# Half-pieces in a hand-interleaved attention and MLP kernel: attention steps counted behind each half of an MLP piece, with a new list of allowances

## The chip, the cores and the metric

One core of one Trainium2 chip runs the whole kernel. The metric is the device time of one execution in microseconds (us). TensorE does the matrix products (PE in the profile; its weight loads are PEld), VectorE (DVE) and ScalarE (ACT) do the elementwise work, GpSimd (POOL) some more of it, and SyncE (SP) mostly issues DMAs.

## What is computed

The reference runs a normalised attention and then an MLP block on its output:

```
q_n, k_n = rmsnorm(q, g_q), rmsnorm(k, g_k)          # (8 batches, 12 heads, 448 tokens, 64)
attn = softmax(q_n @ k_n.T / 8) @ v                  # per batch and head
x = attn, heads side by side                         # (8, 448, 768)
xn = layernorm(x) * g_ln
out = x + relu(xn @ w_ch1) @ w_ch2                   # w_ch1 768 x 3072, w_ch2 3072 x 768
```

## The kernel before

The attention of batch 0 runs first, in an order written out by hand (`ORDER`). After that come eight stages. In stage b (b = 0 to 7) TensorE runs the MLP of batch b and, in between, the attention of batch b + 1; stage 7 has only the MLP. The instructions of each engine run in the order in which Python emits them; nothing reorders them.

**The attention steps.** `attention` (line 529) makes a list of steps, 42 for each stage. Heads are taken in pairs, six pairs to a batch, seven steps to a pair. A step of index i holds the scores of one pair, `scores(p, i)`, and the values of the pair before it, `values(p - 1, i)`. A score step (written S below) is one matmul of 448 columns into a PSUM bank (line 397), which ScalarE turns into E with an exponential (line 413). A value step (V) is four small matmuls of E with v into the banks oA and oB (lines 450 and 452). Step 1 holds two value steps, step 6 the seventh (V6). After V6, `evac_o` (lines 465 to 472) divides on VectorE and frees oA and oB; there is one of each, so the next pair's first V waits for that. The seventh scores of two pairs are made together, as four narrow matmuls into two banks (line 403, written L4). Score banks are two, and from pair 15 (in batch 2) on a third one is used in turn (`score_bank`, line 419). The steps also carry the preparation of later heads: two squares on ScalarE (line 254) and a rounding copy (line 279), sums and scalings on VectorE, DMA transposes and loads on SP.

**The MLP pieces.** `mlp_chunks` yields pieces with a cost. In stages 1 to 7 a piece of the first product ("up", line 775) is 12 matmuls of 256 columns or 24 of 128 columns into one bank, followed by a ReLU on ScalarE (line 777), cost 1280; a piece of the second product (line 797) is 6 matmuls of 384 columns, cost 960. In stage 0 both kinds are 6 matmuls of 384 columns (lines 700 and 711), cost 960. Pieces of cost 0 are VectorE, ScalarE and GpSimd work such as `sums` and `sum3` (line 780), `add` (line 737) and `join` (line 807). An MLP batch is done in two groups: tokens 0 to 255 and then the rest in odd batches, the third block of 128 and then the other two in even batches. The bank pool of the MLP has three buffers.

**The pace.** `run_rest` (line 951) emits one piece, adds its cost to `done`, and then emits attention steps up to `start + (goal - start) * done / (total - 960 * tail)`. `tail` comes from `TAIL` (line 64), so a tail of 17 means that the steps are all out when 17 x 960 of cost is left. Then the layer norm of the next batch follows, one item behind each piece: A (aggregate), N (normalise, on VectorE), X (transpose by DMA, on SP, at the earliest when 10 pieces are left, `DOWN`), R (root). In stages 0 and 1 one of 16 weight sums on VectorE (line 743) also follows a piece, from the last nine pieces of stage 0 on.

Of the kernel before, what the change touches and what calls it, by code (L numbers as in the profile page):

```python
# [8 lines left out]
FP32 = mybir.dt.float32  # L9
# [3 lines left out]
AFT = mybir.ActivationFunctionType  # L13
# [7 lines left out]
NDC, NFF = DM // 128, FF // 128  # L21
# [39 lines left out]
RS_RATIO = 4.0  # L61
HALF, HCOL = NFF // 2, DM // 2
DOWN = 10
TAIL = (13, 17, 17, 17, 17, 17, 17, 0)
FLAG_AT = (6, 30)
E_RING = 9
RING = [(u, n) for u in (4, 6, *range(DMA_UNIT, len(UNITS))) for n in "kq"]
# [20 lines left out]
class _Fast:  # L88
# [603 lines left out]
    def first_mlp(self):  # L692

        nc, sh = self.nc, self.sh
        tiles, xnT, hT = self.tok_tiles(0), self.xnT, self.hS

        def up(f):
            ps = self.ps_m.tile([128, 512], FP32, tag="mlp", name="psH")
            for dc in range(NDC):
                nc.tensor.matmul(ps[:, 0:384], sh.w1[:, dc, ts(f, 128)], xnT[:, dc],  # L700
                                 start=(dc == 0), stop=(dc == NDC - 1))
            nc.scalar.activation(out=hT[:, f], in_=ps[:, 0:384], func=AFT.Relu)

        cur = {}

        def down(t, g, s):
            if s == 0:
                cur["ps"] = self.ps_m.tile([128, 512], FP32, tag="mlp", name="psC")
            ps = cur["ps"][:, 0:HCOL]
            for f in range(6 * s, 6 * s + 6):  # L710
                nc.tensor.matmul(ps, hT[:, f, ts(t, 128)], sh.w2[:, f, ts(g, HCOL)],
                                 start=(f == 0), stop=(f == NFF - 1))
            if s == 3:
                self.add(0, t, g, ps)
                if g and t < 2:
                    self.late.append((0, t, slice(0, DM)))
                elif t == 2:
                    self.store(0, t, slice(g * HCOL, g * HCOL + HCOL))
            elif s == 1:
                self.store_late()  # L720

        for f in range(UP_FIRST, NFF):
            yield 6 * 384 / 2.4, (lambda f=f: up(f))
        for g in range(2):
            for t in range(3):
                for s in range(4):
                    yield 6 * HCOL / 2.4, (lambda t=t, g=g, s=s: down(t, g, s))

    def store_late(self):
        for a in self.late:  # L730
# [23 lines left out]
    def mlp_group(self, b, tiles, end, before=(), after=()):  # L754

        nc, sh = self.nc, self.sh
        w2, w2s, S2 = sh.w2, self.w2s, self.S2
        lo, hi = slice(0, HALF), slice(HALF, NFF)
        t0, n = tiles[0], len(tiles)
        N, k = 128 * n, 4 // n  # L760
        hT = self.hT if n == 2 else self.h1
        last = b == B - 1
        final = last and end
        A1, A2 = (lambda f: hT[:, f, 0:128]), (lambda f: hT[:, f, 128:256])
        B11, B21 = w2[:, lo, 0:HCOL], w2[:, hi, 0:HCOL]
        B22, T3 = w2[:, hi, HCOL:DM], w2[:, lo, HCOL:DM]
        T1, T2, T4 = (w2s[:, i] for i in range(3))
        U, V, W = self.U, self.V, S2.rearrange("p f n -> p (f n)").bitcast(FP32)[:, 0:HCOL]
        bank, half, before = {}, 6 * HCOL / 2.4, list(before)

        def up(f):
            ps = self.ps_m.tile([128, k, N], FP32, tag="mlp", name="psH")
            for i in range(k):
                for dc in range(NDC):
                    nc.tensor.matmul(ps[:, i], sh.w1[:, dc, ts(f + i, 128)], self.xnT[:, dc, 256 - N:256],  # L775
                                     start=(i == 0 and dc == 0), stop=(i == k - 1 and dc == NDC - 1))
            nc.scalar.activation(out=hT[:, f:f + k], in_=ps, func=AFT.Relu)  # L777

        def tt(out, a, c, op=ALU.subtract):
            nc.vector.tensor_tensor(out=out, in0=a, in1=c, op=op)  # L780
# [1 line left out]
        def sum3(i):  # L782
            f = slice(4 * i, 4 * i + 4)
            return 0, lambda: tt(A2(f), A2(f), A1(f))

        def sums(i):
            f, f2 = slice(4 * i, 4 * i + 4), slice(HALF + 4 * i, HALF + 4 * i + 4)
            if n == 1:
                return 0, lambda: tt(S2[:, f], A1(f), A1(f2), ALU.add)
            return 0, lambda: (tt(S2[:, f], A2(f), A2(f2), ALU.add),  # L790
                               tt(A1(f), S2[:, f], A1(f), ALU.add))

        def product(x, a, w, s, start=True, stop=True, c=slice(0, HCOL)):
            if x not in bank:
                bank[x] = self.ps_m.tile([128, 512], FP32, tag="mlp", name="psP")[:, 0:HCOL]
            for f in range(6 * s, 6 * s + 6):
                nc.tensor.matmul(bank[x][:, c], a[:, f], w[:, f, c], start=(start and f == 0),  # L797
                                 stop=(stop and f == HALF - 1))

        run = lambda *a, **kw: [(half, lambda s=s: product(*a, s, **kw)) for s in range(2)]  # L800

        def add(x, t, g):
            return 0, lambda: self.add(b, t0 + t, g, bank[x] if isinstance(x, str) else x)
# [9 lines left out]
                                         nc.scalar if b == B - 1 else nc.gpsimd)  # L813

        for f in range(0, NFF, k):
            yield 6 * 512 / 2.4, (lambda f=f: up(f))
            if before:
                yield 0, before.pop(0)
            if n == 1:
                if f in (16, 20):  # L820
                    yield sums(f // 4 - 4)
                continue
            if f in (4, 8, 12):
                yield sum3(f // 4 - 1)
# [63 lines left out]
            yield done(1)  # L888
            return
        for c in range(0, HCOL, 192):  # L890
            for s in range(2):
                yield half / 2, lambda s=s, c=c: product(f"4{c}", A2(hi), T4, s, c=slice(c, c + 192))
            yield 0, lambda c=c: self.add(b, t0 + 1, 0, bank[f"4{c}"][:, c:c + 192], c, c + 192)
            yield 0, lambda c=c: self.store(b, t0 + 1, slice(c, c + 192), nc.scalar)

# [55 lines left out]
    def run_rest(self):  # L951
        steps, mark, upto = self.steps, self.mark, self.upto
        for b in range(B):
            tail = TAIL[b]
            chunks = list(self.mlp_chunks(b))
            total = sum(c for c, _ in chunks)
            if b + 1 == B:
                for i, (_, emit) in enumerate(chunks):
                    if i == len(chunks) - 55:
                        self.tc.mark_branch_hint_location("general", "LikelyTaken", [ENG.PE, ENG.DVE, ENG.SP, ENG.Activation, ENG.Pool])  # L960
                    emit()
                    if i in FLAG_AT:
                        self.flag(FLAG_AT.index(i))
                break
            start, goal = self.pos, mark[b + 1]
            done, items = 0.0, None
            if b == 0:
                ops, last = self.weight_sums()
            elif b == 1:
                ops += last  # L970
            left = sum(c > 0 for c, _ in chunks)
            for cost, emit in chunks:
                emit()
                if not cost:
                    continue
                left -= 1
# [241 lines left out]
```

## Time and profile before

| | |
|---|---|
| time, median of 3 runs | 590.68 us (589.38 to 590.95) |
| the profiled execution | 591.34 us, of which the span from first to last instruction is 589.8 us |
| TensorE busy | 560.6 us, 95% of the span |
| VectorE, ScalarE, GpSimd busy | 391.3, 373.0, 173.8 us |
| first attention | 0 to 58.6 us of the span |
| stages 0, 1, 2 | from 58.6, 123.2, 197.4 us |
| stages 3, 4, 5 | from 259.9, 333.0, 393.6 us |
| stages 6, 7 | from 466.7, 525.0 us |

The span starts with the first instruction; times inside the profile are counted from there. A busy time of PE joins overlapping matmuls, and a matmul's row is longer than its share of the stream: a matmul of 448 columns has a row of 0.35 us, and the next one starts 0.19 us after it. A PE gap shorter than that overlap does not show as idle time.

### The profile page before, as it was taken

How to read it: one execution, taken by the hardware profiler on the slowest of the kernel's cores; microseconds unless marked ns; L12 is line 12 of the kernel's file. 1: busy time of each engine (PE TensorE's matmuls, PEld its weight loads, DVE VectorE, ACT ScalarE, POOL GpSimd, SP SyncE). 2: the span in 40 equal slices, each digit the busy share in tenths (PEclk: the TensorE clock that was granted, in tenths of full speed). 3: DMA queues.
4: the chain of work that ended last, by engine and by line, in shares of the span. 5: the costliest groups of instructions: out<-in, count | busy, mean ns of one | idle time of the engine just before them, and what ended most of it. 6: DMA issues, size and time to landing. Idle time of an engine off the chain costs nothing.

```text
span 589.8 us, 13476 instructions
## 1 busy us (share of the span) xinstructions
PE 560.6 (95%) x5366; PEld 409.3 (69%) x5366; DVE 391.3 (66%) x832; ACT 373.0 (63%) x693; POOL 173.8 (29%) x196
## 2 busy tenths in 40 slices
PE   3877999999999999999999999999999999999996
PEld 1555566677687867767777767767777777777784
DVE  5798667798768476965868576765868533573424
ACT  5987897448775588738777388738777377323130
POOL 2845433303150511644141421634241410020000
PEclk9999999999999999999999999999999999999999
DMA  8999998839582687959773597949852480030201
GB/s 218 279 209 238 197 208 119 142 110 140 122 129 65 144 123 129 127 140 133 138 118 31 154 137 147 136 126 136 136 90 43 122 107 1 1 108 1 83 0 57
DMA packets 172664, 71.43 MB, mean 121 GB/s; under 512 B 132548, under 2 KB 167556, under 8 KB 172596
## 3 DMA queue, kind: packets, MB, share of 16 engines
q1 hardware_dynamic: 130100, 51.60, 41.5%
q0 software_dynamic: 41552, 18.29, 24.0%
q8 instruction: 43, 0.70, 0.5%
q10 hardware_dynamic: 944, 0.62, 0.5%
q14 instruction: 25, 0.20, 0.1%
HBM read 52.30 MB, written 11.01 MB: 107 GB/s over the span
## 4 chain that ended last, share of the span: by engine, by line
PE 68%; DVE 4%; ACT 2%; DMA 2%; issue 1%; SPq 0%; DVEq 0%; ACTq 0%
PE psP L797 28%; PE psH L775 28%; PE psS L397 5%; PE oA L450 4%; DMA k<-in_k_dram 2%; PE psS L403 1%; PE oB L452 1%; ACT E L413 1%; DVE qn L79 1%; ACT hS L777 1%; DVE ssq L257 1%; DVE x L467 0%; DVE hS L780 0%; ACT khl L254 0%; ACT khl L279 0%
## 5 line engine op out<-in xcount | busy, mean ns | idle before, releaser
L413 ACT ACTIVATE E<-psS,rr_all 128x448 f16<-128x448 f32 x336 | 201.5, 635 | 27.2 <-PE psS L397 23.6
L775 PE MATMUL psH<-xnT,w 128*128 128x256 f16 (+1 forms) x2016 | 216.6, 261 | 0.0
L775 PEld LDWEIGHTS <-w 128*128 128x128 f16 x2016 | 174.8, 98 | 20.5 <-issue 0.9
L777 ACT ACTIVATE hS<-psH 128x512 f16<-128x512 f32 x150 | 90.0, 600 | 121.2 <-PE psH L775 120.5
L797 PEld LDWEIGHTS <-hS 128*128 128x128 f16 x1080 | 100.1, 98 | 62.4 <-issue 5.1
L797 PE MATMUL psP<-w,hS 128*128 128x384 f16 x672 | 123.5, 326 | 0.3 <-DVE x L737 0.3
L397 PE MATMUL psS<-qU,kU 128*128 128x448 f16 x288 | 99.1, 359 | 9.4 <-ACT E L413 6.8
L450 PEld LDWEIGHTS <-E 128*128 128x128 f16 x1008 | 69.8, 98 | 37.5 <-issue 6.3
L271 POOL TENSOR_TENSOR k<-k,gprod 128x896 f32<-128x896 f32 x19 | 40.0, 2105 | 162.5 <-ACT khl L254 107.8
L780 DVE TENSOR_TENSOR hS<-hS 128x512 f16<-128x512 f16 (+1 forms) x119 | 66.1, 563 | 21.2 <-ACT hS L777 19.7
L797 PE MATMUL psP<-w2s,hS 128*128 128x384 f16 (+1 forms) x408 | 70.0, 321 | 0.0
L450 PE MATMUL oA<-v,E 128*128 128x65 f16 x864 | 67.1, 194 | 0.4 <-DVE x L467 0.4
L737 DVE SCALAR_TENSOR_TENSOR x<-psP,rs_all,x 128x384 f32<-128x384 f32 x60 | 36.4, 616 | 31.5 <-PE psP L797 30.2
L452 PE MATMUL oB<-v,E 128*128 128x65 f16 x288 | 52.0, 194 | 0.1
L807 POOL TENSOR_TENSOR x<-x,hS 128x384 f32<-128x384 f32 x21 | 21.4, 1031 | 93.1 <-ACT hS L875 90.9
L465 DVE RECIPROCAL rec_all<-oA 128x6 f32<-128x6 f32 x48 | 9.2, 193 | 58.6 <-PE oA L450 58.5
L212 POOL DMA_DIRECT2D v<-in_v_dram x51 | 39.6, 789 | 6.3 <-PE oB L452 5.4
L397 PEld LDWEIGHTS <-kU 128*128 128x128 f16 x288 | 28.1, 99 | 14.7 <-issue 5.8
L875 ACT ACTIVATE hS<-hS,rs_all 128x384 f32<-128x384 f32 x27 | 14.6, 604 | 33.5 <-DVE hS L780 33.5
L257 DVE TENSOR_REDUCE ssq<-khl 128x14 f32<-128x896 f32 (+1 forms) x24 | 25.5, 1063 | 11.7 <-ACT khl L254 10.8
L452 PEld LDWEIGHTS <-E 128*128 128x128 f16 x336 | 32.7, 97 | 0.5 <-DVE xl L472 0.4
L79 DVE SCALAR_TENSOR_TENSOR qn<-q,rr_all 128x256 f16<-128x256 f32 (+1 forms) x70 | 26.5, 439 | 5.6 <-ACT rr_all L261 5.6
(136 smaller groups left out, 596.3 us busy)
## 6 DMA issues: line engine op xcount, KB each, us to landing
k<-in_k_dram SPq DMA_DIRECT2D x19, 384.0 KB, 4.1
q<-in_q_dram SPq DMA_DIRECT2D x19, 384.0 KB, 3.7
out_dram<-x SPq DMA_DIRECT2D x14, 384.0 KB, 3.0
w<-in_moe_w_ch_dram POOLq DMA_DIRECT2D x3, 1536.0 KB, 14.2
w<-in_moe_w_ch_dram POOLq DMA_DIRECT2D x2, 2304.0 KB, 19.6
out_dram<-x POOLq DMA_DIRECT2D x9, 384.0 KB, 2.9
v<-in_v_dram POOLq DMA_DIRECT2D x51, 64.0 KB, 4.3
qU<-qn SPq DMA_TRANSPOSE x85, 2.6
```

What stands on the lines that cost most here:

```text
L79: nc.vector.scalar_tensor_tensor(out=out, in0=x, scalar=8.0, in1=r.unsqueeze(2).broadcast_to([x.shape[0], g, D]), op0=ALU.mult, op1=ALU.mult)
L212: nc.gpsimd.dma_start(out[:, :, j, 0:D], main[:, :, j])
L271: (nc.vector if u in DVE_KG else nc.gpsimd).tensor_tensor(out=c["t"][1], in0=c["t"][1], in1=sh.gprod.unsqueeze(1).broadcast_to([128, g, D] ...
L397: nc.tensor.matmul(ps[0][:, 0:S], c["main"][:, ts(i, 128)], c["q"][:, ts(h, S)], start=True, stop=True)
L413: nc.scalar.activation(out=o, in_=x[:, 0:S], func=AFT.Exp, scale=self.units[u][3][:, g:g + 1], bias=EXP_BIAS)
L450: nc.tensor.matmul(oA[:, t, cs], E[:, ts(t, 128)], rhs, start=(i == 0 and t == 0), stop=(i == 6 and t == 2))
L452: nc.tensor.matmul(oB[:, cs], E[:, 320:448], rhs, start=(i == 0), stop=(i == 6))
L737: self.nc.vector.scalar_tensor_tensor(out=x, in0=ps, scalar=self.rs[:, b, t:t + 1], in1=x, op0=ALU.mult, op1=ALU.add)
L775: nc.tensor.matmul(ps[:, i], sh.w1[:, dc, ts(f + i, 128)], self.xnT[:, dc, 256 - N:256], start=(i == 0 and dc == 0), stop=(i == k - 1 and ...
L777: nc.scalar.activation(out=hT[:, f:f + k], in_=ps, func=AFT.Relu)
L780: nc.vector.tensor_tensor(out=out, in0=a, in1=c, op=op)
L797: nc.tensor.matmul(bank[x][:, c], a[:, f], w[:, f, c], start=(start and f == 0), stop=(stop and f == HALF - 1))
```

## The change

Each piece with a cost is now a list of two calls, its first and its second half: 6 + 6 or 12 + 12 matmuls of an up piece, 3 + 3 of the others. A half-piece's matmuls stand in the same order and go to the same bank as before. Between the two calls `run_rest` emits attention steps up to the target that belongs to `done + cost / 2`; after the second call it emits up to the same target as before. The ReLU stays behind the second half. `TAIL` goes from 13 to 11 for stage 0, from 17 to 13 for stages 1, 3 and 5, from 17 to 19 for stage 6, and stays at 17 for stages 2 and 4.

```diff
-TAIL = (13, 17, 17, 17, 17, 17, 17, 0)
+TAIL = (11, 13, 17, 13, 17, 13, 19, 0)
...
-        def up(f):
-            ps = self.ps_m.tile([128, k, N], FP32, tag="mlp", name="psH")
-            for i in range(k):
+        def up(f, h):
+            if h == 0:
+                bank["h"] = self.ps_m.tile([128, k, N], FP32, tag="mlp", name="psH")
+            ps = bank["h"]
+            for i in range(h * k // 2, (h + 1) * k // 2):
...
-            nc.scalar.activation(out=hT[:, f:f + k], in_=ps, func=AFT.Relu)
+            if h:
+                nc.scalar.activation(out=hT[:, f:f + k], in_=ps, func=AFT.Relu)
...
-            for f in range(6 * s, 6 * s + 6):
+            for f in range(3 * s, 3 * s + 3):
                 nc.tensor.matmul(bank[x][:, c], a[:, f], w[:, f, c], start=(start and f == 0),
                                  stop=(stop and f == HALF - 1))
...
-            yield 6 * 512 / 2.4, (lambda f=f: up(f))
+            yield 6 * 512 / 2.4, [lambda f=f, h=h: up(f, h) for h in range(2)]
...
             for cost, emit in chunks:
-                emit()
                 if not cost:
+                    emit()
                     continue
+                for i, call in enumerate(emit):
+                    call()
+                    if i + 1 < len(emit):
+                        upto(int(min(goal, start + (goal - start) * (done + cost / 2) / (total - 960 * tail))))
                 left -= 1
```

The same halving is made in `first_mlp` for stage 0. In the last group of stage 7 the four pieces of cost half / 2 become eight of half / 4, with the same matmuls in the same order.

On TensorE the built orders of stages 2, 3 and 6 read as follows (u: up matmuls, p: matmuls of the second product, with their number; S, V and L4 as above; one line for two pairs).

```
stage 2 before  u24 S u24 SVV SV u24 SV SV u24 SVV u24 SSVV u24 SV SV p6 SV SV p6V L4
                p6 S p6 SVV SV p6 SV p6 SV SV p6V p6 SSVV u12 SV SV u12 SV SV u12V L4
                u12 SSVV u12 SV SV u12 SV SV u12V S p6 SVV SV p6 SV u12 SV SV u12V L4
                p12 u36 p60
stage 2 after   u24 S u12 SVV u12 SV u12 SV u12 SV u12 SV u12V u12 S u12 SVV u12 SV u12 SV p3 SV p3 SV p6V L4
                p3 S p6 SVV p3 SV p3 SV p6 SV p3 SV p3V p6 S p3 SVV u6 SV u6 SV u6 SV u6 SV u6V L4
                u12 S u6 SVV u6 SV u6 SV u6 SV u6 SV u6V u6 S p3 SVV p3 SV p6 SV u6 SV u6 SV u6V L4
                u6 p12 u36 p60
stage 3, last pair, before   u12 SSVV u12 SV p6 SV p6 SV u12 SV u12V L4 p12 u36 p60
stage 3, last pair, after    p6 S p6 u6 SVV u6 SV u12 SV p6 SV p6 SV u12V L4 u24 p60
stage 6, last pairs, before  u12 SSVV u12 SV SV u12 SV u12 SVV p6VVV p6V u12VV u12V p12 u36 p60
stage 6, last pairs, after   u6 S u6 SVV u6 SV u6 SV u6 SV u6 SV u6V u6VV u6V u6V p3V p6V p3V u24 p12 u36 p60
```

The order of GpSimd's instructions is the same in both kernels; on SP one DMA transpose of stage 6 stands behind two others instead of before them; VectorE has a few `add` and `sums` at other places among the preparation.

More of the change, by code (lines that the diff above doesn't have):

```diff
@@ L694, in first_mlp, with up @@
         nc, sh = self.nc, self.sh
-        tiles, xnT, hT = self.tok_tiles(0), self.xnT, self.hS
-        def up(f):
-            ps = self.ps_m.tile([128, 512], FP32, tag="mlp", name="psH")
-            for dc in range(NDC):
+        tiles, xnT, hT, cur = self.tok_tiles(0), self.xnT, self.hS, {}
+        def up(f, i):
+            if i == 0:
+                cur["h"] = self.ps_m.tile([128, 512], FP32, tag="mlp", name="psH")
+            ps = cur["h"]
+            for dc in range(3 * i, 3 * i + 3):
                 nc.tensor.matmul(ps[:, 0:384], sh.w1[:, dc, ts(f, 128)], xnT[:, dc],
                                  start=(dc == 0), stop=(dc == NDC - 1))
-            nc.scalar.activation(out=hT[:, f], in_=ps[:, 0:384], func=AFT.Relu)
-        cur = {}
+            if i:
+                nc.scalar.activation(out=hT[:, f], in_=ps[:, 0:384], func=AFT.Relu)
         def down(t, g, s):
@@ L709, in down @@
             ps = cur["ps"][:, 0:HCOL]
-            for f in range(6 * s, 6 * s + 6):
+            for f in range(3 * s, 3 * s + 3):
                 nc.tensor.matmul(ps, hT[:, f, ts(t, 128)], sh.w2[:, f, ts(g, HCOL)],
                                  start=(f == 0), stop=(f == NFF - 1))
-            if s == 3:
+            if s == 7:
                 self.add(0, t, g, ps)
@@ L718, in down @@
                     self.store(0, t, slice(g * HCOL, g * HCOL + HCOL))
-            elif s == 1:
+            elif s == 3:
                 self.store_late()
         for f in range(UP_FIRST, NFF):
-            yield 6 * 384 / 2.4, (lambda f=f: up(f))
+            yield 6 * 384 / 2.4, [lambda f=f, i=i: up(f, i) for i in range(2)]
         for g in range(2):
@@ L726, in first_mlp @@
                 for s in range(4):
-                    yield 6 * HCOL / 2.4, (lambda t=t, g=g, s=s: down(t, g, s))
+                    yield 6 * HCOL / 2.4, [lambda t=t, g=g, s=s: down(t, g, s)
+                                           for s in (2 * s, 2 * s + 1)]
     def store_late(self):
@@ L769, in mlp_group @@
         bank, half, before = {}, 6 * HCOL / 2.4, list(before)
-        def up(f):
-            ps = self.ps_m.tile([128, k, N], FP32, tag="mlp", name="psH")
-            for i in range(k):
+        def up(f, h):
[3 more added lines that the diff above has]
+            for i in range(h * k // 2, (h + 1) * k // 2):
                 for dc in range(NDC):
@@ L795, in product @@
                 bank[x] = self.ps_m.tile([128, 512], FP32, tag="mlp", name="psP")[:, 0:HCOL]
-            for f in range(6 * s, 6 * s + 6):
+            for f in range(3 * s, 3 * s + 3):
                 nc.tensor.matmul(bank[x][:, c], a[:, f], w[:, f, c], start=(start and f == 0),
                                  stop=(stop and f == HALF - 1))
-        run = lambda *a, **kw: [(half, lambda s=s: product(*a, s, **kw)) for s in range(2)]
+        run = lambda *a, **kw: [(half, [lambda s=s: product(*a, s, **kw) for s in (2 * s, 2 * s + 1)])
+                                for s in range(2)]
         def add(x, t, g):
@@ L890, in mlp_group @@
         for c in range(0, HCOL, 192):
-            for s in range(2):
-                yield half / 2, lambda s=s, c=c: product(f"4{c}", A2(hi), T4, s, c=slice(c, c + 192))
+            for s in range(4):
+                yield half / 4, lambda s=s, c=c: product(f"4{c}", A2(hi), T4, s, c=slice(c, c + 192))
             yield 0, lambda c=c: self.add(b, t0 + 1, 0, bank[f"4{c}"][:, c:c + 192], c, c + 192)
@@ L960, in run_rest @@
                         self.tc.mark_branch_hint_location("general", "LikelyTaken", [ENG.PE, ENG.DVE, ENG.SP, ENG.Activation, ENG.Pool])
-                    emit()
+                    for call in emit if isinstance(emit, list) else [emit]:
+                        call()
                     if i in FLAG_AT:
@@ L972, in run_rest @@
             for cost, emit in chunks:
-                emit()
                 if not cost:
+                    emit()
                     continue
+                for i, call in enumerate(emit):
+                    call()
+                    if i + 1 < len(emit):
+                        upto(int(min(goal, start + (goal - start) * (done + cost / 2) / (total - 960 * tail))))
                 left -= 1
```

## The prediction, made before the changed kernel ran

> **What bounds the kernel now.** I read the page's first lines, then busy time by stage, then who makes TensorE wait, then the timelines around the longest waits.
>
> ```profile
> PE 560.6 (95%) x5366; PEld 409.3 (69%) x5366; DVE 391.3 (66%) x832; ACT 373.0 (63%) x693; POOL 173.8 (29%) x196
> ```
>
> TensorE is busy for 95% of the span. The table by stage (length, then PE, PEld, DVE and ACT busy, clock, DMA share) shows where the rest is:
>
> ```profile
> 58.60:123.20 64.60, 63.32 (x547) 40.26 (x545) 47.06 (x99) 44.47 (x85) 22.31 (x23) 1.00 0.97 168
> 123.20:197.40 74.20, 73.61 (x674) 54.27 (x672) 56.14 (x112) 50.41 (x92) 17.91 (x18) 1.00 0.58 109
> 197.40:259.90 62.50, 60.76 (x639) 45.27 (x637) 43.93 (x94) 43.42 (x81) 21.42 (x25) 1.00 0.92 132
> 259.90:333.00 73.10, 73.10 (x673) 54.28 (x672) 49.25 (x102) 49.45 (x91) 24.12 (x27) 1.00 0.64 116
> 333.00:393.60 60.60, 60.06 (x639) 45.03 (x637) 42.00 (x94) 43.44 (x81) 21.79 (x25) 1.00 0.85 136
> 393.60:466.70 73.10, 73.10 (x674) 54.29 (x673) 49.26 (x102) 49.45 (x91) 24.11 (x27) 1.00 0.58 103
> 466.70:525.00 58.30, 58.19 (x628) 43.97 (x627) 28.76 (x74) 32.20 (x60) 8.26 (x12) 1.00 0.32 55
> ```
>
> Length less PE busy is 1.28, 0.59, 1.74, 0, 0.54, 0 and 0.11 us for stages 0 to 6: 4.26 us in all. The change only reorders matmuls in these stages, so this, with about 0.17 us more at each wait (the tail of the last matmul's row, counted as busy), is all it can win. Stages 3 and 5, whose allowance it alters, have nothing to give. The waits of stages 0 to 6 by cause:
>
> ```profile
> PE psS L397 <- ACT E L413: 2.1, 5, 0.5
> PE psS L397 <- DVE kU L365: 0.9, 1, 0.9
> PE oA L450 <- DVE x L467: 0.4, 1, 0.4
> PE psP L797 <- DVE x L737: 0.3, 1, 0.3
> ```
>
> Half is score steps that wait for a bank, which an exponential frees. Stage 2, first PE and then ACT:
>
> ```profile
> 210.04 0.19 PE L452 MATMUL oB<-v,E 128*128 128x65 f16 x1
> 210.78 0.35 PE L397 MATMUL psS<-qU,kU 128*128 128x448 f16 x1 [0.54 <-ACT E L413]
> ```
>
> ```profile
> 206.39 0.60 ACT L777 ACTIVATE hS<-psH 128x512 f16<-128x512 f32 x1 [0.76 <-PE psH L775]
> 206.89 0.94 ACT L254 ACTIVATE khl<-k 128x896 f32<-128x896 f32 x1
> 207.73 0.63 ACT L413 ACTIVATE E<-psS,rr_all 128x448 f16<-128x448 f32 x1
> 208.24 0.95 ACT L254 ACTIVATE qn<-q 128x896 f32<-128x896 f32 x1
> 210.07 0.65 ACT L413 ACTIVATE E<-psS,rr_all 128x448 f16<-128x448 f32 x1
> ```
>
> ScalarE sits idle for 0.76 us until a ReLU's matmuls are done; then two squares and the exponentials come behind it, and the sixth S finds no bank: it starts 0.71 us after the exponential that frees one. From the 210.04 row V's last matmul should be followed after 0.03 us, so the wait is 0.70 us of the stream. Starts in sequence give ACT's rate: an exponential every 0.52, a square or rounding copy 0.85, a ReLU 0.48 us. PE: S 0.19, V 0.12, twelve up matmuls 1.31 (0.67 at 128 columns), three p 0.49.
>
> **The change part by part.** Splitting costs no instruction: matmul counts, order and banks of the MLP stay. An alternation is free: where the timelines change between up, S, V and p without a wait, the next matmul starts on schedule (S at 209.77, V at 209.96). What moves is the place of S and V, on average a quarter piece earlier, and with them their DVE, ACT, SP and POOL work. GpSimd's order stays. On SP one transpose of xn (1.2 us) of stage 6 comes behind two others; group 2 needs it eight p pieces (8 x 0.97 us) later, so I count nothing; without that cover it would cost those two, 2.5 us.
>
> 1. Stages 2 and 4, second pair: S steps no longer come as SVSV but 0.67 and 0.49 us apart, and the ReLU ahead of the squares comes earlier. Walking the new order by the rates above, ACT begins the squares about 1.5 us earlier and every bank is free in time: -0.70 each, **-1.4**.
> 2. The same stages, next boundary: V6 L4 p3 S p6 S V has p3 where p6 stood. V waits for evac_o, behind the rounding copy's followers on VectorE (1.09 and 1.08 us rows); 0.49 us less cover, up to 0.35 late: **+0.7** (0 to +0.7).
> 3. Stage 2, fourth pair. Here ACT waits for a load:
>
> ```profile
> 223.39 0.95 ACT L254 ACTIVATE qn<-q 128x896 f32<-128x896 f32 x1 [1.43 <-DMA k<-in_k_dram]
> ```
>
> The load's issue hangs on an SP chain from the stage's start, not on PE. S steps that come earlier only meet the same late square. Before, waits here cost 0.70 and 0.15; by the walk the fifth S then waits 1.55 and L4 0.56: at most +1.26; 0 if the load lands earlier as well. I take nearer the walk, **+0.9**.
> 4. End of stage 2: L4's second bank 0.36 late becomes 0.2, and the p that waited 0.51 for an add has six more up matmuls (0.65) ahead of it: **-0.7**.
> 5. Stage 4, pairs 4 and 6: the same loads, now just late: 0 to +0.6, **+0.4**.
> 6. Stage 1: a bank wait of 0.34 goes (S spaced by u6). The V at 135.69 waits 0.52 and its oB 0.22 for a VectorE that works without a pause from the stage's start. With allowance 11 stage 0's last V6 comes two pieces (1.9 us) later against stage 1; less an add and a reduce that no longer lie in the chain, VectorE enters stage 1 some 0.75 us later, which eats most of the p6 (0.97) that now stands ahead of that V: -0.3 to -1.1, **-0.5**.
> 7. Stage 0: the first S waits until 62.54 for a VectorE copy. It now comes after 15 up matmuls, not 18; 3 x 0.16 = 0.49 more wait, unless it is taken out of a later wait for ACT (0.45 us at 78.7): **+0.25**. Two L4 that followed SVV at once now have a half-piece between: 0.16 each, **-0.3**.
> 8. Stages 1, 3, 5, the end. In stage 3 the VectorE chain runs so:
>
> ```profile
> 316.91 0.20 DVE L465 RECIPROCAL rec_all<-oA 128x6 f32<-128x6 f32 x1 [0.63 <-PE oA L450]
> 319.75 1.02 DVE L646 SCALAR_TENSOR_TENSOR xn<-x,stat,gln 128x768 f16<-128x768 f32 x1
> 321.86 1.67 DVE L780 TENSOR_TENSOR hS<-hS 128x512 f16<-128x512 f16 x4
> 324.08 0.88 DVE L780 TENSOR_TENSOR hS<-hS 128x512 f16<-128x512 f16 x2 [0.55 <-ACT hS L777]
> ```
>
> evac_o to A takes 2.8 us, N 1.0, six sums 0.42 each; product 6 needs them in thirds. Before, L4 p12 u36 p12 lay between V6 and product 6 (8.3 us). Now it is L4 u24 p12, 5.1 us, and 6.4 to its ninth matmul, which needs the fifth sum: 2.8 + 1.0 + 5 x 0.42 = 5.9, after a start that two adds and a reduce ahead (1.14 + 1.08) push 0.5 behind V6 and 0.1 of hand-over: 6.5. About 0.2 late, three times: **+0.6** (0 to +5.7, if adds and reduce lay wholly behind V6).
> 9. Stage 6: V6 and the next V are u6 (0.65) apart, where p6 (0.97) was and the V was 0.22 late: **+0.3**. Its larger allowance gives layer norm two pieces more, which nothing there waits for.
>
> Sum: -1.4 + 0.7 + 0.9 - 0.7 + 0.4 - 0.5 + 0.25 - 0.3 + 0.6 + 0.3 = +0.25 us. The profiled execution is 591.34 us (589.8 of span, 1.54 around it), 0.66 above the median; the sum is a difference, so I add it to the median: 590.68 + 0.25, about 591.0.
>
> **The rivals.** *Bunching is the whole cause.* Then every wait for a bank or oA of stages 0 to 6 goes: 3 x 0.70, 0.45, 0.34, 0.74, 0.3, 0.36, 0.15 and 0.51 = 4.95, less terms 7's 0.49 and 9's 0.3: 590.68 - 4.1 = 586.6. For it: four of the five bank waits follow two S that stand 0.31 us apart. Against it: one follows a late load, one a busy VectorE.
>
> *The shorter allowance bites.* In stages 1, 3 and 5 product 6 waits for the sums. If the reduce and half of the adds lie behind V6, the chain starts 1.6 us after it, and each stage waits 1.3 instead of 0.2: 591.0 + 3.3 = 594.3. It decides from a start 0.4 us after V6 on. For it: 3.2 us of cover are gone, and VectorE is busy 49.3 of 73.1 us. Against it: it idled 0.63 and 0.55 us here.
>
> *The banks are too few.* The 0.54 gap at 210.78 comes again at 346.38 in stage 4, and the change adds no bank. If the spacing does not matter, term 1 and the bank part of term 4 (0.16) fall away: 591.0 + 1.6 = 592.6. For it: ACT's work in that pair (two squares, a rounding copy, eight exponentials, two ReLUs, 7.7 us) exceeds PE's 7.15 (48 up matmuls 2.68, 12 p 1.95, six S and V 1.88, V6 and L4 0.64). Against it: it idles just ahead. The Trainium skill's Perfetto Trace Analysis, section Optimization Strategy, says that a gap which repeats on the engine that should be saturated can mean too little PSUM or SBUF for the next tile. The repeat agrees with that; whether spacing helps no run here shows.
>
> **How the numbers follow.** A measurement of this kernel can tell about 0.3% (1.8 us) from no change. The forecast gets 0.5; bunching 0.22 and faster; the allowance 0.18 and slower; the banks 0.1, at the edge, which I split between same and slower. So faster 0.22, same 0.55, slower 0.23. The low ends of terms 2, 3, 5 and 8 give 590.68 - 2.35 = 588.3; the range reaches a little beyond, to 588.0, and up to 594.0, near the allowance rival: outside lie most of bunching's chance and the far half of the allowance's.
>
> **What would show it.** Right: no 0.54 wait in the second pairs of stages 2 and 4, but a wait in stage 2's fourth pair behind the load, a longer first S in stage 0, and product 6 in stages 1, 3 and 5 a few tenths late on VectorE. PE idle of stages 0 to 6 stays near 4.3 us. Wrong: stage 2 shorter by over 1.5 us, or stages 3 and 5 longer by 1 us each.

## The result, and the profile after

The changed kernel takes 589.24 us (median of 13 runs, 588.15 to 590.25) where the kernel before takes 590.95 us (13 runs, 589.38 to 592.47): the ratio is 0.997, with a 95% interval of 0.9959 to 0.9981. In a second comparison it is 0.9963 (0.995 to 0.9975). The change therefore gains about 2 us (0.3%), and both intervals leave out a ratio of 1. The prediction said 591.0, a change of +0.25 us and no difference: the time went the other way.

The page after, the line that answers to the first one shown of before:

```profile
PE 557.1 (95%) x5366; PEld 407.3 (69%) x5366; DVE 381.9 (65%) x832; ACT 378.7 (65%) x693; POOL 174.9 (30%) x196
```

The table by stage of the changed kernel (columns as before: length, then PE, PEld, DVE, ACT and POOL busy, clock, DMA share, GB/s):

```profile
57.30:122.50 65.20, 62.94 (x548) 40.06 (x546) 45.72 (x99) 44.84 (x85) 21.45 (x23) 1.00 0.99 170
...
196.60:256.80 60.20, 59.96 (x637) 44.93 (x636) 42.03 (x94) 43.74 (x81) 21.35 (x25) 1.00 0.92 137
256.80:330.00 73.20, 73.20 (x675) 54.35 (x673) 45.66 (x102) 50.81 (x91) 25.03 (x27) 1.00 0.62 116
330.00:389.80 59.80, 59.73 (x638) 44.74 (x637) 42.03 (x94) 44.07 (x81) 21.43 (x25) 1.00 0.93 138
```

Stage 0 is longer (65.2 for 64.6), stage 2 shorter by 2.2 and stage 4 by 0.7; stage 3 still has nothing to give. In this profile the first attention, whose code the change does not touch, also ends 1.26 us earlier; that is taken up under "Run or program?". Who makes TensorE wait in stages 0 to 7 of the changed kernel:

```profile
PE psS L397 <- DVE kU L365: 1.3, 1, 1.3
PE psS L397 <- ACT E L413: 0.6, 2, 0.3
PE psS L403 <- ACT E L413: 0.6, 1, 0.6
PE oA L450 <- DVE x L467: 0.4, 1, 0.4
```

The first and third line belong to stage 0. The five waits of a single S (line 397) for a bank have become two, and neither lies in stage 2 or 4. The second pair of stage 2, ACT and then PE, where the sixth S used to wait:

```profile
203.99 0.60 ACT L782 ACTIVATE hS<-psH 128x512 f16<-128x512 f32 x1 [0.16 <-PE psH L779]
204.48 0.94 ACT L254 ACTIVATE khl<-k 128x896 f32<-128x896 f32 x1
205.32 0.63 ACT L413 ACTIVATE E<-psS,rr_all 128x448 f16<-128x448 f32 x1
205.84 0.60 ACT L782 ACTIVATE hS<-psH 128x512 f16<-128x512 f32 x1
206.32 0.96 ACT L254 ACTIVATE qn<-q 128x896 f32<-128x896 f32 x1
```

```profile
208.43 0.35 PE L397 MATMUL psS<-qU,kU 128*128 128x448 f16 x1
...
209.23 0.35 PE L397 MATMUL psS<-qU,kU 128*128 128x448 f16 x1
```

ScalarE's idle time ahead of the ReLU is 0.16 us where it was 0.76, the square of k starts 7.9 us after the stage's start (9.5 before), a ReLU stands between the squares, and S steps 0.80 us apart find a bank each time.

### The profile page after: what moved, and what is told of

Its sections match the earlier page's. It is cut to its first block, busy times and chain, and to the rows that moved or that the text cites. A ratio compares the mean times of both kernels' runs of the same rounds, so it can differ in the third digit from the quotient of the medians.

```text
span 586.6 us, 13477 instructions
## 1 busy us (share of the span) xinstructions
PE 557.1 (95%) x5366; PEld 407.3 (69%) x5366; DVE 381.9 (65%) x832; ACT 378.7 (65%) x693; POOL 174.9 (30%) x196
## 4 chain that ended last, share of the span: by engine, by line
PE 78%; DVE 8%; ACT 3%; DMA 2%; issue 1%; SPq 0%; DVEq 0%; ACTq 0%
PE psH L779 30%; PE psP L802 28%; PE psS L397 7%; PE oA L450 4%; PE psH L702 3%; PE psC L712 2%; PE oB L452 2%; PE psS L403 1%; DVE w2s L745 1%; DMA q<-in_q_dram 1%; ACT E L413 1%; DVE stat L625 1%; DVE khl L282 1%; DVE ssq L257 1%; DVE x L467 1%
## 5 line engine op out<-in xcount | busy, mean ns | idle before, releaser
L779 PE MATMUL psH<-xnT,w 128*128 128x256 f16 (+1 forms) x2016 | 225.8, 261 | 0.0
L779 PEld LDWEIGHTS <-w 128*128 128x128 f16 x2016 | 172.7, 98 | 24.0 <-issue 4.8
L802 PE MATMUL psP<-w,hS 128*128 128x384 f16 x672 | 126.8, 326 | 0.0
L397 PE MATMUL psS<-qU,kU 128*128 128x448 f16 x288 | 102.0, 356 | 9.4 <-ACT E L413 6.0
L785 DVE TENSOR_TENSOR hS<-hS 128x512 f16<-128x512 f16 (+1 forms) x119 | 56.8, 484 | 22.3 <-ACT hS L782 20.8
L813 POOL TENSOR_TENSOR x<-x,hS 128x384 f32<-128x384 f32 x21 | 23.4, 1127 | 84.4 <-ACT hS L881 83.8
L282 DVE TENSOR_TENSOR khl<-k,khl 128x896 f16<-128x896 f32 x19 | 20.7, 1091 | 25.9 <-ACT khl L279 25.9
```

Of the source, the lines that this page charges most:

```text
L397: nc.tensor.matmul(ps[0][:, 0:S], c["main"][:, ts(i, 128)], c["q"][:, ts(h, S)], start=True, stop=True)
```

## The experiments

Four theories were set against each other. Spacing: S and V no longer come in bunches in stages 2 and 4. Allowance: the new list does it. Load: a load of q in stage 2 lands at a time that differs from run to run. Port: VectorE and GpSimd collide. Stage lengths below run from the first up matmul of a stage to that of the next, in the profiled run; stage 0 from its first matmul after the first attention. The ratios are those of the run times, each to the kernel before on the same chip; the experiments ran on three chips.

| kernel | stage 0 | 1 | 2 | 4 | 6 | ratio to before (95%) |
|---|---|---|---|---|---|---|
| before | 64.62 | 74.20 | 62.49 | 60.56 | 58.30 | 1 |
| changed | 65.21 | 74.04 | 60.28 | 59.84 | 58.62 | 0.997 (0.9959 to 0.9981) |
| e1 halves, old list | 65.49 | 74.03 | 61.07 | 60.64 | 58.79 | 0.9986 (0.9974 to 0.9999) |
| e2 new list, whole pieces | 65.85 | 74.27 | 62.78 | 60.57 | 59.27 | 1.005 (1.003 to 1.0069) |
| e4 halves in 1 to 5 | 64.61 | 73.25 | 61.50 | 59.84 | 58.30 | 0.9948 (0.9931 to 0.9965) |
| f1 changed, again | 65.20 | 74.03 | 61.26 | 59.84 | 58.61 | 0.9963 (0.995 to 0.9975) |
| f2 changed, load ahead | 65.20 | 74.04 | 60.12 | 59.83 | 58.62 | 0.9958 (0.9945 to 0.9971) |
| f3 before, load ahead | 64.61 | 74.20 | 61.52 | 61.51 | 58.30 | 0.9985 (0.9975 to 0.9996) |
| f4 e4 and load ahead | 64.61 | 73.25 | 59.98 | 59.84 | 58.30 | 0.9943 (0.993 to 0.9956) |
| g1 before, GpSimd later | 64.62 | 74.19 | 61.70 | 60.56 | 58.30 | 0.9978 (0.9964 to 0.9993) |
| g2 f4, allowance 11 in 3, 5 | 64.61 | 73.25 | 59.95 | 59.84 | 58.30 | 0.9959 (0.9945 to 0.9973) |
| g3 halves in 2 and 4 alone | 64.62 | 74.20 | 61.70 | 60.21 | 58.30 | 0.9967 (0.9955 to 0.9979) |
| g4 f4, old list | 64.62 | 74.03 | 60.43 | 59.84 | 58.30 | 0.9944 (0.9926 to 0.9962) |

Stages 3 and 5 take 73.1 us in all of them but e2 (73.30 each) and g2 (73.81 and 73.57).

Diffs are against the changed kernel, those of f3 and g1 against the kernel before.

**The two parts of the change, each alone.** e1 keeps the half-pieces and takes back the list:

```diff
-TAIL = (11, 13, 17, 13, 17, 13, 19, 0)
+TAIL = (13, 17, 17, 17, 17, 17, 17, 0)
```

> The half-pieces everywhere, with the old list of allowances. Spacing theory (the gain is the spacing of S and V in stages 2 and 4, which the allowances do not touch): stages 2 and 4 take 60.3 and 59.8 us, as in the changed kernel, stages 3 and 5 stay at 73.1, stage 0 keeps the longer first S (about 65.1); in all 2 us less than before, ratio 0.996 to 0.997, the changed kernel's or a little better. Allowance theory (the new list brings the gain): the time of before, ratio 1.000. Load theory (about half of stage 2's 2.2 us is a load of q that happened to land earlier in one profiled run): stage 2 comes out anywhere from 60.3 to 61.5, ratio 0.997 to 0.999.

e2 keeps the list and emits no attention step between the halves:

```diff
-                    if i + 1 < len(emit):
+                    if i + 1 < len(emit) and b in ():
```

> The new list of allowances, with no attention step between the two halves of a piece; stages 2 and 4 are then those of before. Spacing theory: stages 2 and 4 take 62.5 and 60.6 us again, with the 0.54 us gap behind the second pair; stages 3 and 5 stay at 73.1, or each lose up to 1.3 us if the shorter allowance leaves product 6 waiting; ratio 1.000 to 1.004. Allowance theory: the gain is kept, ratio 0.997. Load theory: stage 2 between 61.5 and 62.5, ratio 0.998 to 1.000.

The halves alone gain 0.8 us; the list alone costs 3 us, more than either theory had asked for; together they gain 1.7 to 2.2. e1's stages 2 and 4 are each 0.8 us longer than those of the changed kernel, though TensorE's order in them is the same: in its profile the load treated below landed late in both. The waits of e2 show where the list costs with whole pieces:

```profile
PE psS L397 <- ACT E L413: 3.0, 6, 0.9
PE oA L450 <- DVE x L467: 1.6, 2, 1.0
```

Its losses lie in stage 0 (+1.23 us; three S wait for ScalarE there) and in stage 6 (+0.97 us; a V behind V6 waits 1.0 us for VectorE). In stages 2 and 4 the waits of 0.71 us in the second pair are all there again. So the allowance theory falls as a cause of the gain in stages 2 and 4; the list as a whole suits the halves only.

**Half-pieces in stages 2 and 4 alone** (g3), with the old list, as in e1, and:

```diff
-                    if i + 1 < len(emit):
+                    if i + 1 < len(emit) and b in (2, 4):
```

> Half-pieces in stages 2 and 4 alone, everything else as before. Spacing theory: stage 2 takes 60.3 to 61.5 us (by the load of q), stage 4 59.8 to 60.6, the rest is before's: 2.0 to 2.8 us less, ratio 0.995 to 0.9965, more than the whole change brings. Allowance theory: no gain without the new list, ratio 1.000.

0.9967: these two stages bring what the whole change brings, if a little less than was expected. Stage 4 takes 60.21 us, as expected; stage 2 takes 61.70, 0.2 more than expected, with the latest load of all profiles with halves. There is no wait for a bank in the second pair of either.

**Stages 0 and 6 as before the change** (e4): half-pieces in stages 1 to 5 and TAIL = (13, 13, 17, 13, 17, 13, 17, 0).

> Half-pieces in stages 1 to 5 with their new allowances; stages 0 and 6 as before the change (whole pieces, allowances 13 and 17). In the changed kernel these two stages lost 0.59 and 0.32 us. Spacing theory, with these losses read as what stages 0 and 6 really cost: 0.9 us less than the changed kernel, ratio to the kernel before 0.995 to 0.996, stage 0 at 64.6 and stage 6 at 58.3 us. If instead stage 0's later end is what lets stage 1 begin with less VectorE work open, stage 1 is longer by some 0.5 us and the time is that of the changed kernel, 0.997.

0.9948, below the changed kernel's 0.997 and 0.9963, though the intervals overlap. Stages 0 and 6 get back 0.60 and 0.32 us. What was not expected is stage 1: 73.25 us, a further 0.79 less. In the changed kernel stage 1 begins with more of VectorE's work left over from stage 0, its first `evac_o` ends 13.6 us after the stage's start, and it has waits of 0.49, 0.20 and 0.22 us; in e4 `evac_o` ends at 12.8 us and of the waits 0.10 us is left.

**The load of q in stage 2.** e4 and the changed kernel have the same order in stage 2, but their lengths differ by 1.2 us. In e4 ScalarE waits 2.36 us for the load, where the first profile of the changed kernel has 1.12:

```profile
222.32 0.95 ACT L254 ACTIVATE qn<-q 128x896 f32<-128x896 f32 x1 [2.36 <-DMA q<-in_q_dram]
```

e4's fifth S then waits for the bank, in the list of its waits in stage 2:

```profile
PE psS L397 <- ACT E L413: 1.1, 1, 1.1
```

Against the stage's start, the last piece of q lands at 24.46 us in the changed kernel, 25.23 in e1, 25.44 in f1, 25.70 in e4 and 25.88 in g3; the fifth S is 0, 0.75, 0.96, 1.21 and 1.39 us late. The piece is issued within 0.44 us in these five; from issue to landing it takes 2.8 to 3.8 us. (In the row that the prediction shows, the profile names a load of k; the landing just before that square starts, at 25.84 us for 25.99, is the last piece of q.) To take the load out of the question, f2, f3 and f4 issue it ahead of the two transposes of the left rows of q (on the sync queue, some 2.5 us earlier):

```diff
-        (12, "z"), (15, "x"), (16, "y"), (18, "Y"))
+        (12, "z"), (15, "x"), (16, "y"), (23, "Y"))
```

> The changed kernel unaltered, a second time, beside kernels that differ in one thing from it. Spacing theory alone (waits are set by the order): stage 2 takes 60.3 us again and the fourth pair's waits are 0.19 and 0.33 us again. Load theory (the last piece of q in stage 2 lands between 24.5 and 26.1 us after the stage's start, by chance, and the fifth S of the fourth pair starts after it): stage 2 takes 60.3 to 61.7 us, and for a landing at 25.7 us the fifth S waits 1.2 us, as it did with half-pieces in stages 1 to 5 alone. Ratio to the kernel before 0.996 to 0.998 in both.

> The changed kernel, with the load of the next q issued ahead of the two transposes of the left rows of q on the sync queue instead of behind them: 2.5 us earlier in stages 1 to 5. Load theory: the square of q in stage 2's fourth pair starts at about 22.3 us after the stage's start, straight behind the square of k and its rounding, whatever the landing; the fifth S and L4 lose their waits; stage 2 takes 59.8 us and stage 4 59.8, that is 0.5 to 1.7 us less than in the changed kernel, ratio 0.994 to 0.996. Rival: the two transposes, now 1.9 us later, become late for the next unit's first S, which then waits up to 1.9 us in each of stages 1 to 5, ratio 0.998 to 1.01. If the load does not matter: ratio 0.997.

> The kernel before, with the same load moved ahead in the same way. Load theory: in stage 2's fourth pair the waits of 0.70 and 0.24 us go, since in stage 4, where the square of q starts at 24.5 instead of 26.0 us, they are not there; if the 0.45 and 0.51 us waits near the end of stage 2 hang on it too, stage 2 loses 1.9 us and equals stage 4's 60.6. So 0.9 to 1.9 us less than before, ratio 0.997 to 0.9985; the 0.70 us wait in the second pair stays in both stages. Spacing theory, by which S steps in a bunch cost their wait whenever the square comes: 0.70 stays in the fourth pair as well, ratio 0.999 to 1.000.

> Half-pieces in stages 1 to 5 with their new allowances, stages 0 and 6 as before the change, and the load of q ahead of the transposes. Load and spacing together: stage 1 at 73.25 us, stages 2 and 4 at 59.8, stages 3 and 5 at 73.1, stages 0 and 6 as in the kernel before; about 1 us less than the same without the load ahead, ratio 0.992 to 0.994. If the earlier load only moves a wait to the transposes: 0.995 or more.

f1 shows the spread: the same program, 61.26 instead of 60.28 us, and a wait of 0.96. In f2 and f4 stage 2 takes 60.12 and 59.98 us, and all of the fourth pair's waits for an exponential are gone. A small part of f2's rival came true: the transposes now land later, and the fourth pair's first S waits for them, 0.28 us in f2, 0.13 in f4 and most in g4 (described below):

```profile
PE psS L397 <- DMA qU<-qn: 0.4, 1, 0.4
```

f4 has the lowest ratio of all, 0.9943, though its interval overlaps those of e4 and g4, as f2's overlaps f1's: the run times alone do not show the gain of the earlier load, the stage lengths do. In f3 the fourth pair's first wait goes as the load theory says, and the two waits near the end of stage 2 stay: those do not hang on the load. And its stage 4 is 0.95 us longer than in the first profile of before, in code that is the same there but for the load. That led to the next cause.

**VectorE against GpSimd.** The kernel before was profiled again (e3).

> The kernel before, profiled a second time, to see what changes from run to run by itself. Spacing theory: stage 2 is 62.5 us again, the last piece of q lands about 25.9 us after the start of stage 2 again, since a load's path is the same in each run. Load theory: it lands up to 1.4 us earlier and stage 2 is shorter by up to 1.2 us. In both, the first attention, whose code the change does not touch, shows by its end (58.6 us before, 57.3 us in the changed kernel) how far the start alone moves between runs.

Stage 2 was 62.49 us again, but stage 4 took 61.53 instead of 60.56, with two waits at its end (0.45 and 0.51 us) that are those of stage 2. In the first profile of before, stage 2 has these rows ahead of its two waits:

```profile
237.44 2.09 POOL L271 TENSOR_TENSOR k<-k,gprod 128x896 f32<-128x896 f32 x1 [14.75 <-DVE xl L472]
237.45 2.37 DVE L780 TENSOR_TENSOR hS<-hS 128x512 f16<-128x512 f16 x1
```

Stage 4 of the same profile, without the two waits, has:

```profile
372.07 2.39 POOL L271 TENSOR_TENSOR k<-k,gprod 128x896 f32<-128x896 f32 x1 [13.78 <-DVE xl L472]
372.07 0.42 DVE L780 TENSOR_TENSOR hS<-hS 128x512 f16<-128x512 f16 x1
```

and in a third profile of before (h1), where stage 4 has them:

```profile
372.67 2.09 POOL L271 TENSOR_TENSOR k<-k,gprod 128x896 f32<-128x896 f32 x1 [13.78 <-DVE xl L472]
372.68 2.36 DVE L780 TENSOR_TENSOR hS<-hS 128x512 f16<-128x512 f16 x1
...
376.13 0.95 ACT L279 ACTIVATE khl<-k 128x896 f16<-128x896 f32 x1 [1.12 <-DVE ssq L257]
```

GpSimd's product of k and VectorE's sum both become free to start when `evac_o` is done, within 10 ns of each other. One of them runs at its own length (0.42 or 2.09 us) and the other is stretched until behind it (2.39 or 2.36 us). Six profiles keep the old order in stages 2 and 4 (before, e2, e3, f3, h1, h2), which makes twelve such meetings: the sum is long in nine, and the two waits stand in those nine stages and in none of the other three. Where the sum is the loser, the reduction of k's squares, the rounding copy on ScalarE, the exponentials behind it and L4 follow about a microsecond late. The Trainium skill's page SBUF — State Buffer, section "SBUF: two separate sides", states that VectorE and GpSimd share a port pair as an exclusive lock for a whole instruction, also against a VectorE operation with two inputs in SBUF; these rows agree with it (0.42 us becomes 2.36 beside one of 2.09).

This meeting is not the only one. In the first profile of before, twelve VectorE rows exceed the median of their line and shape by 0.8 us or more, 12.3 us over in all, and every one of them ends 0.28 or 0.29 us behind a GpSimd instruction; in the first profile of the changed kernel there are four, 5.0 us over. Most of the fall in VectorE's busy time, from 391.3 to 381.9 us with the same 832 instructions, is this. Only for the meeting in stages 2 and 4 was it tested that TensorE pays for it: g1 delays GpSimd a little, in the kernel before:

```diff
+            if UNITS[u][0] in (3, 4, 5, 6):
+                nc.gpsimd.tensor_copy(out=c["t"][1][:, 0:1], in_=c["t"][1][:, 0:1])
             (nc.vector if u in DVE_KG else nc.gpsimd).tensor_tensor(
```

> The kernel before, with a copy of one 64-element group onto itself put on GpSimd ahead of each product of k with the gains (line 271) of batches 3 to 6, so that this product starts a little later. In the traces of before it starts within 10 ns of VectorE's next sum of hS (line 780) near 39 to 40 us of stages 2 and 4; where GpSimd is first the sum takes 2.36 us instead of 0.42, and L4 (0.45 us) and a p matmul (0.51 us) wait later. Port theory: with GpSimd reliably second, the sum takes 0.4 us in both stages, both waits go in each run, stage 2 takes 61.5 and stage 4 60.6 us; 1.0 to 1.5 us less than before, ratio 0.9975 to 0.9985. Load theory (those two waits come from the late square of q): stage 2 stays at 62.5 us, ratio 1.000.

```profile
237.81 0.50 DVE L782 TENSOR_TENSOR hS<-hS 128x512 f16<-128x512 f16 x1
238.11 2.15 POOL L273 TENSOR_TENSOR k<-k,gprod 128x896 f32<-128x896 f32 x1
```

Ahead of these rows stands the copy, 0.24 us from 237.80. The sum takes 0.50 us, both waits are gone in stage 2 although the load of q is late there (26.01 us), stage 4 is 60.56, and the ratio is 0.9978 (0.9964 to 0.9993): the port theory holds, and one small copy brings the kernel before about 1.3 us. In the changed kernel, and in all eleven profiles with halves in stages 2 and 4, this collision is gone too. There evac_o ends 0.9 us before the square of k does, and the sum is over when GpSimd starts (first profile of after, stage 2):

```profile
234.75 0.43 DVE L785 TENSOR_TENSOR hS<-hS 128x512 f16<-128x512 f16 x1
...
235.62 2.09 POOL L271 TENSOR_TENSOR k<-k,gprod 128x896 f32<-128x896 f32 x1 [14.57 <-ACT khl L254]
```

**The allowance of stages 3 and 5.** g2 goes on to 11 there, g4 back to 17 in stages 1, 3 and 5; both are otherwise f4.

> Half-pieces in stages 1 to 5, stages 0 and 6 as before, load ahead, and an allowance of 11 instead of 13 in stages 3 and 5. L4 is then followed by u6 and p12 ahead of product 6 instead of u24 and p12. Chain as measured in the changed kernel (the fifth sum is done 5.91 us after V6, product 6's ninth matmul starts 6.38 us after it): 18 up matmuls of 0.109 us fewer, 1.96 us, make it want the sum at 4.42 us, so product 6 waits 1.5 us in each of the two stages: 74.6 us each, ratio to before 0.998 to 1.000 where allowance 13 gave 0.994. If the cover were as thin as the prediction had it (0.2 us late already at 13), it would be 2.0 us each; if VectorE's chain moved forward with the earlier pieces, nothing.

> Half-pieces in stages 1 to 5, load ahead, and the old list of allowances throughout (13, then 17). Beside the same with the new allowances of 13 in stages 1, 3 and 5 (ratio 0.9943) it shows what those bring. Spacing theory: stages 3 and 5 are at 73.1 us in either case, since TensorE never waits there, stage 1 at 73.2 to 73.7, stages 2 and 4 at 60.0 and 59.8: ratio 0.9943 to 0.995. Allowance theory: 0.6 to 0.9 us worse, ratio 0.9955 or more.

In g2 product 6 does wait for VectorE's sums, 0.69 us in stage 3 and 0.46 in stage 5, and never in f4; the 1.5 us expected were too much, since four of the six sums of stage 3 now lie ahead of `evac_o`, where all six lay behind it in the changed kernel. In stage 3 the list of waits has:

```profile
PE psP L802 <- DVE hS L785: 0.5, 1, 0.5
```

g4 equals f4 in stages 3 and 5, is 0.78 us longer in stage 1 (74.03 us, where the spacing theory had 73.2 to 73.7), and cannot be told from f4 by its time. So stage 1 needs two things for its 73.25 us: stage 0 as it was before, and the allowance of 13. With halves and only the first of these (g4) or only the second (the changed kernel) it takes 74.03 to 74.04.

**Run or program?** Four more profiles were taken, since the first attention had ended 1.2 us earlier in some kernels.

> The kernel before once more. Chance theory: the first up matmul of stage 0 starts at 51.5 to 52.0 or at 52.7 to 53.0 us with no regard to the program, and stage 4 takes 60.56 or 61.5 us as VectorE or GpSimd is first by 10 ns. Program theory: 52.7 us again for the former. Stage 2 is 62.5 us in both, if GpSimd is first there each time.

> As the third profile of the kernel before: by chance 51.5 to 52.0 or 52.7 to 53.0 us for the first up matmul of stage 0, by program 52.7; stage 4 60.56 or 61.5 us.

> Half-pieces in stages 1 to 5 and the load in its old place, a second time: by program 52.8 us for the first up matmul of stage 0 as before, by chance either value. Stage 2 takes 60.0 to 61.7 us by the landing of q, stages 1 and 4 73.25 and 59.84 or a little more.

> The same with the load ahead, a second time: by program 51.6 us, by chance either value. Stage 2 takes 59.9 to 60.4 us, stages 1 and 4 73.25 and 59.84.

The first up matmul of stage 0 starts at 53.10, 51.89, 52.44 and 52.22 us in h1 to h4, and before started it at 52.79 and 52.68: h2 shows that this differs between runs of one program. That the program has no part in it is not shown. The early times (51.53 to 52.22) are those of h2 and of all profiles of the changed kernel, e1, f2, f4 (h4 is f4 again), g2 and g4; the late ones (52.44 to 53.10) are those of the other three of before and of all of e2, e4 (h3 is e4 again), f3, g1 and g3. Up to about a microsecond of a difference in time could therefore come from ahead of stage 0; the stage lengths, on which the causes here rest, begin behind it. h3 takes 61.34 us in stage 2 and 60.23 in stage 4, h4 60.03 and 59.83, about as expected. Stage 4 of before took 60.56 us once and 61.53 three times; stage 2 took 62.49, 62.49, 62.77 and 60.98, the last with an early load (25.28 us) and with a sum of 0.43 us.

## Why the prediction was wrong, point by point

Measured in the first pair of profiles, stage by stage, by the time from one matmul's start to the next; where a term depends on the run, the mean over the profiles stands with it.

| step | forecast | measured |
|---|---|---|
| 1 second pairs, stages 2 and 4 | -1.4 | -1.41, in every kernel with halves there |
| 2 the V behind L4 | +0.7 | +0.2 |
| 3 fourth pair of stage 2 | +0.9 | -0.53; mean of six profiles with halves against five of before's order, all with the load in its old place, +0.4 |
| 4 end of stage 2 | -0.7 | -0.96 in stage 2, 0 in stage 4; against before's four profiles -0.96 in three of four in each of the two stages, so -1.4 on average |
| 5 stage 4, the loads | +0.4 | 0; mean of six +0.3 |
| 6 stage 1 | -0.5 | -0.16 |
| 7 stage 0 | -0.05 | +0.59 |
| 8 stages 1, 3, 5, the end | +0.6 | 0 |
| 9 stage 6 | +0.3 | +0.32 |

The prediction's own sign of being wrong came: stage 2 is shorter by 2.2 us, where it allowed 1.5. Steps 1 and 9 were right in mechanism and in size. The walk along ScalarE's queue was right too: it put the squares about 1.5 us earlier, and that of k came 1.56 us earlier (7.92 us after the stage's start for 9.48).

Step 4 is the one that failed by its cause. The prediction read the 0.51 us wait of p as one for an add that more cover would hide, and the bank as late by 0.36. In fact both follow from the collision of line 271 with line 780, which the trace shown had in stage 2 (the sum's row is 2.37 us) and, by chance, not in stage 4. With the halves it is gone in both stages: 0.96 us in stage 2, and as much in stage 4 in three of before's four profiles. On average that is -1.4 us for the -0.7 forecast, 0.7 us of the 2 that were missed; steps 2, 3 and 8 were each 0.5 or 0.6 us too dear, and steps 6 and 7 together 1.0 us too cheap.

Step 3's mechanism was right and its size depends on the run: at a landing of 25.70 us (e4) the fifth S waits 1.21 and L4 0.56 us (0.10 of which stands ahead of every L4), where the walk gave 1.55 and 0.56 for the landing of the first profile of before, 25.84. At that landing these rows would give some +0.9, which is an estimate, so the size was right for its condition. In the profiled run of after the load landed early, and the step came out on the other side. The forecast took one landing for a fixed time.

Step 2 was bounded too cautiously: the V's own wait is 0, only oB waits 0.23, and the 0.12 us that p lost behind L4 go. Step 8 summed rows on VectorE that overlap: from `evac_o` to the fifth sum takes 5.60 us, where 5.9 was summed from the rows, and the chain starts 0.31 us behind V6 and not 0.5. The fifth sum is done 5.91 us after V6, product 6's ninth matmul comes at 6.38, so 0.47 us were to spare, as g2 bears out (18 up matmuls fewer, and it waits). Step 7 named the longer first S (1.51 for 1.03 us, as computed); what was wrong is that a later wait for ScalarE would absorb it: two such waits are left, 0.80 and 0.47 us. Step 6 named the price of stage 0's later end, but it ate all but 0.16 us; e4, without it, gains 0.95.

By the mean of the profiles of each, stages 2 and 4 gain 1.41 and 1.45 us, stage 0 costs 0.59, stage 1 gains 0.16 and stage 6 costs 0.32: -2.1 us in all, which agrees with both measured ratios (-1.8 and -2.2 us). The agreement owes something to the landings in the changed kernel's two profiles (24.46 and 25.44 us): by the mean of all six profiles with halves and the load in its old place, stages 2 and 4 gain 0.99 and 1.19 us, and the sum is -1.4. The spans of the first two profiles differ by 3.2 us, since 1.26 of it lies in the first attention.

Of the rivals, bunching was the nearest: the waits behind S steps in pairs went. It was not the whole cause, since the 0.96 us at the end of a stage were the port's, and the load's part stayed. That the banks are too few is refuted: the repeated 0.54 us gap went with the same banks. The shorter allowance did not bite at 13 with halves; with whole pieces (e2) it did, in stages 3 and 5 by the 0.2 us that step 8 had.

What stays open is why the load's time to landing differs by a microsecond between runs, and by how much each of stage 0's waits is the halves' or the allowance's: alone the halves make that stage 0.87 us longer (e1) and the allowance 1.23 (e2), together 0.59. Open too is which half of step 1's mechanism does it: S steps come further apart and ScalarE's squares start earlier in the same kernels, and no run has the one without the other.

## What to carry to other kernels

Before a wait is charged to the order of the work, look for a row that is several times as long as its twins, and at what the other engine does beside it; which of two instructions loses when they start within 10 ns of each other can change from run to run, and a small delay put ahead of one of them settles it. Sum a chain by start-to-start times, not by rows, and ask of each load in it how far its landing moves between runs. A change of pace pays where TensorE waits: give it to those stages alone.

## What the runs showed of the hardware

A sum on VectorE was stretched from 0.42 to 2.36 us by GpSimd, and a product on GpSimd from 2.09 to 2.39 us by VectorE, and the recorded starts do not tell who wins. GpSimd's record starts first in all twelve meetings, by 4 to 8 ns, and VectorE's sum is nevertheless the quick one in three of them. At 6 ns both outcomes occur: in h2's stage 2 the sum takes 0.43 us, in e3's 2.36. The expectations speak of GpSimd being first where the sum is long; the traces show only that the sum is long.

In the first attention TensorE works more slowly for a time, and when that ends differs by run. The same S, of 448 columns, in the first profile of before and of after:

```profile
23.11 0.56 PE L397 MATMUL psS<-qU,kU 128*128 128x448 f16 x1
```

```profile
22.34 0.35 PE L397 MATMUL psS<-qU,kU 128*128 128x448 f16 x1
```

Its row is 0.56 us in the one and 0.35 in the other, though the granted clock is 1.00 in both there. The first up matmul of stage 0 starts at 51.5 to 53.1 us in the eighteen profiles, and the slow S steps split them cleanly. In nine profiles the last S with a row of over 0.5 us starts at 22.7 to 24.4 us, and the up matmul at 52.44 or later; in the other nine it starts at 20.12 us or earlier, and the up matmul at 52.22 or earlier. The two groups are 1.06 us apart on average. What ends the slow stretch was not tried.
